# Slot 10 of a main batch: the load of the fourth operand's sums ahead of the loads of the sixth operand and of v

## The chip, the cores and the metric

The kernel runs on one core of one Trainium2 chip. The metric is the device time of the whole program in microseconds (us), the median of several runs. TensorE (PE) does the matrix products, VectorE (DVE), ScalarE (ACT) and GpSimd (POOL) the elementwise work, and SyncE (SP) issues nearly all DMA transfers from one queue that it works through in order.

## What is computed

Attention with a threshold, for 8 batches, 8 heads, 576 positions and head size 64, and behind it a gated feed-forward block over the 4608 tokens that come out:

```python
scores = scale * np.matmul(q, k.transpose(0, 1, 3, 2))
thresh = np.max(scores, axis=-1, keepdims=True) - tau
scores = np.where(scores >= thresh, scores, -1000000000.0)
scores = scores - np.max(scores, axis=-1, keepdims=True)
attn = np.exp(scores)
attn = attn / (np.sum(attn, axis=-1, keepdims=True) + 1e-09)
attn_out = np.matmul(attn, v)                  # (B,H,S,D), then turned to x: (B*S, H*D)
g = x @ w_gate
silu = g * (1.0 / (1.0 + np.exp(-g)))
val = x @ w_val
out = silu * val @ w_out                       # d_model 512, d_ff 1536
```

All numbers are float32.

## The kernel before

**Slots.** From the second batch on the attention of a batch is cut into 12 slots: four pairs of heads with three slots each. The loop at the end of the kernel function counts them with `s`; `b` is the batch, `kk = s % 12` the slot in it, and `x` (0, 1 or 2) the slot within its pair. A slot starts on PE with the scores (`slot_scores`, L1989, written to the tile `sc`). With `x == 1`, PE first multiplies the attention of the pair before with v (`attend`, L2088, tile `xa`). DVE, ACT and POOL find maxima, exponentials, masks, sums and transposes of the scores (`slot_rest`, L2010 to L2066). The rest of PE's time in a slot is filled with the feed-forward part of the batch before (`block_part`): first gates and values (L1109), then the output product.

**The output product from the third chunk on** is the class `Deep`. A product is split by nested schemes of seven products in place of eight, so that operands are sums and differences of blocks. Its steps are spread over slots: `p1` and `gates_end` in slot 9, `p2` and `p7` in slot 10, `p6` and `p4` in slot 11, `p5` in slot 0 and `p3` in slot 1 of the next batch. Each step is one call of `nested` (L1711): seven groups of matmuls into `px` or `py`. The token side has sums that POOL makes from `hall` (L925). On the weight side three of the seven operands have sums that don't fit on the chip. They stand in `stream_hbm` (operands 5, 3 and 4 counted from 0) and are loaded for each chunk by `stream` (L1612). Operand 3, which is the fourth, is the one of this case: `p7` asks for its load, its place is `middle` (a part of the tile `big`), which `p7` itself still reads through the sums of its token side, and `p4` in the next slot multiplies with it. Operand 2 has its sums in `sixth_hbm`; `sixth` (L1617) loads them into `xall`, for `p3`.

**Other loads around it.** `prepare_next` loads q and k of the next pair in slots with `x == 1` (L419, four transfers each); DVE and POOL scale and transpose them (L2138, L2135, L2141), and the scores of the next pair need them two slots later. `prepare_v` loads v of the pair that is in work (`load_v`, L456, four transfers of 144 KB); its reader is `attend` three slots later. A one-element memset on DVE (`clear_first`, L1022) comes ahead of it, and the load waits for that. `ship` stores finished outputs (L1772). `next_flow` loads the weight sums of gates and values for the next chunk (L1040, 1280 or 1024 KB each).

**The order.** The kernel writes each engine's instructions in an order that a small planner finds while the program is built. `Plan.job` takes an engine, an assumed duration and what the job depends on (other jobs, or points of planned time such as `plan.t`); an engine's next job is the one that can start first, by rank and by when it is ready. SP counts as an engine here. A dependency that is only a planned time gives an order and no wait; true waits come from the tiles that are read and written. In slot 10 the calls come in this order: `prepare_next`, `prepare_v`, and then `block_part` with `p2` and `p7`. In `p7`:

```python
mark = plan.t
self.inner_sums(4, self.a21, flow_end, self.ready["s1"], mark)
...
stream(3, False, m)
deep_jobs[2] = sixth(self.c, mark)
```

Here `m` is `mark` and a fixed pipeline time of 0.22. So SP gets, in slot 10: four loads of q, four of k, four of v, one store of outputs, the sixth operand, the fourth operand's sums, and behind them, when PE has done `p6`, the first of the loads L1040.

Of the kernel before, what the change touches and what calls it, by code (L numbers as in the profile page):

```python
# [27 lines left out]
class Plan:  # L28
# [12 lines left out]
    def job(self, eng, took, fn, *deps, rank=1, lag=0.0, moves=0.0):  # L41
        j = Job(eng, took, fn, rank, lag, moves)
        for d in deps:
            if isinstance(d, Job) and d.end is None:
                d.then.append(j)
                j.waits += 1
            elif d is not None:
                j.ready = max(j.ready, self.after(d, eng) if isinstance(d, Job) else d + self.HOP)
        if not j.waits:
            self.open[eng].append(j)  # L50
        return j
# [93 lines left out]
def kernel(  # L145
# [63 lines left out]
    vall = const.tile([P, 2 * NJ * D], F32, name="vall")  # L209
# [641 lines left out]
    plan = Plan()  # L851
# [62 lines left out]
    DEEP = 2  # L914
# [106 lines left out]
    def clear_first(place, *deps):  # L1021
        return job("DVE", 0.07, lambda: nc.vector.memset(place[:, 0:1], 0.0), *deps, rank=0)  # L1022
# [69 lines left out]
    class Group:  # L1092
# [89 lines left out]
        def p7(self):  # L1182
            m = self.mul(self.b, self.w[6], x_block(self.c, 1, 0), False, self.u1, *self.w_deps[6], *ready_x[self.c][3])
            u, old = turn_of(u_bufs)
            self.u2_buf = u
            self.u2 = job("ACT", 0.55, lambda: nc.scalar.activation(u.ap, self.b.rows(), AF.Copy, scale=0.5), m, *old, rank=0)
            tt, eng, took = (dve_tt, "DVE", 0.62) if tail[0] else (pool_tt, "POOL", 1.3)
            self.g2 = job(eng, took, tt(u.ap, u.ap, self.s.ap, ALU.add), self.u2, self.s5, rank=1)
            self.s.jobs = [self.g2]
# [328 lines left out]
    deep_jobs = [[] for _ in operands]  # L1518
# [41 lines left out]
    def sixth_place(c):  # L1560
        return xall[:, c % 2 * XW:(c % 2 + 1) * XW]
# [47 lines left out]
    def stream(o, in_tail, *deps):  # L1609
        w = (2 if o == 4 else 3) * QW  # L1610
        place = place_of(o, in_tail)
        deep_jobs[o] = [thirds[o], job("SP", 0.1, lambda: nc.sync.dma_start(out=place[:, 0:w], in_=stream_hbm[STREAMED.index(o)][:, 0:w]),  # L1612
                                       *streamed_kept[o], *deps, lag=1.6, moves=2.2)]

    def sixth(c, *deps):
        place = sixth_place(c)
        return [*deep_jobs[2][:1], job("SP", 0.1, lambda: nc.sync.dma_start(out=place, in_=sixth_hbm), *sixth_kept, *deps, lag=1.6, moves=1.9)]  # L1617
# [12 lines left out]
    def last_of_sixth(*deps):  # L1630
        b11, b12, b21, b22 = quarters(operands[2])
        deep_jobs[2] = [job("POOL", 1.0, pool_tt(b12, b22, b12, ALU.subtract), *sixth_kept, kept_third[2], *deps, rank=3)]
# [7 lines left out]
    class Deep:  # L1640
# [229 lines left out]
        def p7(self):  # L1870
            self.y, deps = self.pair("py")
            m = self.nested(6, self.y, True, *deps)
            mark = plan.t
            self.inner_sums(4, self.a21, flow_end, self.ready["s1"], mark)
            self.inner_sums(2, self.a12, free_place, self.ready["s4"], m, *(j for x in sevens[False] for j in x.jobs))
            stream(3, False, m)
            deep_jobs[2] = sixth(self.c, mark)
            self.c7 = self.copies(self.spaces[1], self.y, m, *u_list[1].jobs, *u_list[2].jobs, *u_list[3].jobs)

        def p6(self):  # L1880
# [265 lines left out]
    def prepare_v(seg, *deps):  # L2146
        seg["vj"] = job("SP", 1.7, lambda: load_v(seg), *deps, lag=2.3, moves=2.6)
# [42 lines left out]
    def gv_steps(n, before_attend=False):  # L2190
        for x in range(n):
            holding[0] = before_attend and x >= n - (HELD if state["c"] >= DEEP else 2)
            next(state["gv"])
        holding[0] = False

    def out_steps(n):
        for _ in range(n):
            if not state["run"]():
                state["run"] = None

    NS = NU3 * NP
    LAST_GV, LAST_PLAIN = 9, 8
    HELD = 4
    GV = {1: 3, 2: 6, 3: 4, 4: 6, 5: 7, 6: 3, 7: 5, 8: 7, 9: 0}
    GV_FIRST = {1: 5, 2: 8, 3: 2, 4: 5, 5: 7, 6: 2, 7: 5, 8: 7, 9: 0}
# [16 lines left out]
    def block_part(b, kk):  # L2222
        s = (b - 1) * NS + kk
        if s == 0:
            state["gv"] = chain(*(plain_group(0, g, u_bufs) for g in range(IN_HEAD, NF2)), *(plain_group(1, g, n_bufs) for g in range(NF2)))
        if s <= NS:
            gv_steps(PLAIN.get(s, 0))
            if s == 2:
                first, state["run"] = outputs(0)
                first.half_sums(plan.t)  # L2230
            elif s == LAST_PLAIN:
                next(state["gv"], None)
            out_steps(CH0.get(s, 0))
            return
        c = b - 1
        if c == DEEP and kk == 0:
            deepen_sixth(plan.t, *summed)
        if kk < 2 and state["run"]:
            out_steps((CH if c - 1 < DEEP else CD).get(kk, 0))
        if kk in GV:  # L2240
            if kk == 1:
                state["gv"], state["c"] = gates_and_values(c), c
                if c > DEEP:
                    deepen_x(c, *(j for js in streamed_kept.values() for j in js))
            gv_steps((GV_FIRST if c == 1 else GV)[kk], kk % NU3 == 0)
            if c == DEEP and kk == 2:
                for o in (4, 2):
                    keep_third(o, plan.t, *summed)
                last_of_sixth(plan.t)
                for o in STREAMED:  # L2250
                    last_of_streamed(o, plan.t)
            if c == DEEP and kk <= len(NESTED):
                deepen(NESTED[kk - 1], plan.t, *(j for js in plain_stores.values() for j in js), *summed)
            if kk == LAST_GV:
                next(state["gv"], None)
                begin_outputs(c)
                if c < DEEP:
                    out_steps(1)
                    end_gates()
        if kk >= LAST_GV:  # L2260
            out_steps((CH if c < DEEP else CD).get(kk, 0))
# [5 lines left out]
    for s, (n, x) in enumerate((n, x) for n in range(len(halved)) for x in range(NU3)):  # L2267
        seg = halved[n]
        i, t = seg["i"], seg["tiles"][x]
        b, kk = s // NS + 1, s % NS  # L2270
        if x == 1 and n > 0:
            attended = attend(halved[n - 1])
        pss, mark = slot_scores(seg, t)
        if s == 0:
            next(last, None)
            attend_tile()
            next(last, None)
            flip()
            plan.t += 2.4
            plan.free.update(DVE=2.0, ACT=2.5)  # L2280
        elif s == 1:
            box = []
            m = pe(1.0, lambda: attend_tile(lambda *y: box.extend(y)))
            j = job("ACT", 0.27, box[1], m, rank=0)
            banks[taken[id(box[0])][0]].jobs.append(j)
            give_back(box[0])
            next(last, None)
            store_last(0, j)
        if s == 1:
            prepare_v(seg)  # L2290
        at_, pooled, max_by_act = (kk, POOLED, MAX_BY_ACT) if b > DEEP else (s, FIRST_POOLED, FIRST_MAX_BY_ACT)
        slot_rest(seg, t, pss, mark, pooled.get(at_, 0), at_ in max_by_act, 1 if x == NU3 - 1 else 2)
        if x == 1 and n > 0:
            for place, load in held:
                load(clear_first(place, behind_scores[0]))
            held.clear()
        if x == (1 if n >= NP else 0) and n + 1 < len(halved):
            prepare_next(i + 1, plan.t, n >= 2 * NP)
        if x == 1 and n > 0:
            prepare_v(seg, clear_first(vall, attended, behind_scores[0]))  # L2300
        if s == 0:
            joins = rest_of_weights()
        block_part(b, kk)
        if 2 <= s < 6:
            output_sums(s - 2, plan.t, *joins)
        if s in WS:
            g, place = WS[s]
            weight_sums(g, place, plan.t, *joins, stores.get({2: 0, 3: 1, 4: 3, 5: 4}.get(g)))
        if 10 <= s < 10 + NF2:
            g = s - 10  # L2310
            weight_part(g, summed_g[g], plan.t)
        if s > NS and x and (g := (s - NS) * (NU3 - 1) // NU3) < NF2:
            store_plain(g, parts[g], plan.t)
            store_nested(g, plan.t)
        if s in STREAM_AT:
            deepen_streamed(STREAM_AT[s], plan.t, *(j for js in (*plain_stores.values(), *nested_stores.values()) for j in js), *summed)
# [70 lines left out]
```

## Time and profile before

| what | us |
|---|---|
| median of 3 runs | 1353.04 |
| lowest and highest of them | 1350.48, 1359.38 |
| the profiled execution, its own time | 1355.35 |
| its span from first to last instruction | 1353.6 |
| PE busy in the span | 1336.0 |
| DVE, ACT, POOL busy | 1066.3, 894.9, 776.2 |

The profiled execution is 2.31 us above the median of the runs. Its span is 1.75 us shorter than its own time; that is what lies around the first and the last instruction. Engines work beside each other, so the busy times don't add up. An engine line such as `L1711 ... px<-wo,hall` names the line of the kernel, the tile that is written and the tiles that are read. SPq is the stream of DMA issues of SP; the time of such a line is that of the issue, and the time to landing is given apart. A main batch takes about 145.5 us: the scores of slot 10 start at 667.33, 813.08 and 1104.07 us, for instance, in the second, third and fifth of the batches that the change touches.

### The profile page before, as it was taken

The page shows a single profiled execution, that of the slowest core. Times are in us where ns is not written, and L with a number is a line of the kernel's source. Part 1 is how long each engine was busy: PE and PEld are TensorE (multiplying, and loading weights), DVE is VectorE, ACT ScalarE, POOL GpSimd, SP SyncE. Part 2 cuts the span into 40 slices and gives each one's busy share as a digit, 9 for nine tenths or more (in the row PEclk, how much of TensorE's full clock was granted, in tenths as well). Part 3 has the DMA queues.
Part 4 walks back from the last instruction along what each step waited for, and adds up shares of the span by engine and source line. Part 5 has one row for each costly group of instructions (what it writes and reads, how often), then busy time and mean ns, then how long its engine had stood idle before and what let it go on. Part 6 is the DMA issues. An engine that isn't in the chain of part 4 may idle for free.

```text
span 1353.6 us, 40310 instructions
## 1 busy us (share of the span) xinstructions
PE 1336.0 (99%) x15914; PEld 1119.7 (83%) x15914; DVE 1066.3 (79%) x2860; ACT 894.9 (66%) x2315; POOL 776.2 (57%) x870
## 2 busy tenths in 40 slices
PE   9999999999999999999999999999999999999998
PEld 7777777787788878888888888887888889999998
DVE  7788898878887787888878887888788876686686
ACT  6888776777755777677767776778677774330330
POOL 2687397565685659655984689556965595000000
PEclk9999999999999999999999999999999999999999
DMA  8753324456557544746264636563464627524621
GB/s 190 194 184 100 75 61 130 127 150 174 149 180 219 174 109 107 213 131 194 60 197 148 211 97 194 158 212 71 145 202 132 185 65 251 201 96 168 207 83 31
DMA packets 216140, 202.11 MB, mean 149 GB/s; under 512 B 166800, under 2 KB 184208, under 8 KB 205200
## 3 DMA queue, kind: packets, MB, share of 16 engines
q1 hardware_dynamic: 212032, 198.62, 49.6%
q8 instruction: 126, 2.06, 0.6%
q10 hardware_dynamic: 3920, 0.92, 0.3%
q14 instruction: 62, 0.51, 0.1%
HBM read 172.36 MB, written 27.13 MB: 147 GB/s over the span
## 4 chain that ended last, share of the span: by engine, by line
PE 86%; POOL 6%; DMA 3%; DVE 2%; issue 1%; SPq 1%; ACT 0%; DVEq 0%; POOLq 0%
PE pb L1109 18%; PE pa L1109 12%; PE sc L1989 9%; PE xa L2088 9%; PE px L1711 9%; PE pe L1109 6%; PE po L1416 6%; PE pe L1294 4%; DMA big<-stream_hbm 2%; PE py L1711 2%; PE pv L1341 2%; POOL big L925 2%; PE pg L1341 2%; PE sc L1294 2%; POOL hall L925 2%; PE py L1720 2%
## 5 line engine op out<-in xcount | busy, mean ns | idle before, releaser
L2037 DVE SCALAR_TENSOR_TENSOR pall<-sc,th,pall 128x288 f32<-128x288 f32 x504 | 244.5, 514 | 41.7 <-ACT pall L2035 22.5
L1109 PE MATMUL pb<-xall,big 128*128 128x256 f32 x1152 | 273.9, 381 | 0.0
L2035 ACT ACTIVATE pall<-sc,nm 128x288 f32<-128x288 f32 x504 | 232.5, 497 | 33.3 <-DVE pall L2037 33.0
L1109 PEld LDWEIGHTS pb<-xall,big 128*128 128x128 f32 x1152 | 215.0, 190 | 30.7 <-issue 2.7
L2066 DVE STREAM_TRANSPOSE pall<-pall 128x576 f32<-128x576 f32 x252 | 188.4, 764 | 23.6 <-ACT pall L2064 15.6
L2064 ACT ACTIVATE pall<-pall,ri 128x288 f32<-128x288 f32 x388 | 179.0, 527 | 33.9 <-DVE ri L2052 33.0
L1109 PE MATMUL pa<-xall,big 128*128 128x256 f32 x768 | 183.1, 381 | 0.0
L925 POOL TENSOR_TENSOR hall<-hall,tmp 128x512 f32<-128x512 f32 x80 | 102.1, 1278 | 106.7 <-DVE hall L1164 87.0
L1109 PEld LDWEIGHTS pa<-xall,big 128*128 128x128 f32 x768 | 143.3, 190 | 21.6 <-issue 2.5
L2010 DVE TENSOR_REDUCE mx<-sc 128x2 f32<-128x576 f32 x168 | 126.0, 750 | 43.8 <-PE sc L1989 43.3
L925 POOL TENSOR_TENSOR big<-big 128x128 f32<-128x128 f32 (+3 forms) x174 | 128.7, 747 | 44.0 <-ACT big L1216 22.4
L1989 PE MATMUL sc<-kT,qT 64*32 64x288 f32 (+1 forms) x5376 | 144.8, 345 | 1.1 <-DVE pall L2037 1.1
L1989 PEld LDWEIGHTS sc<-kT,qT 64*32 64x32 f32 x5376 | 95.3, 106 | 50.0 <-issue 9.3
L2088 PE MATMUL xa<-pall,vall 64*32 64x288 f32 x4032 | 128.8, 404 | 0.4 <-PE px L1711 0.4
L2088 PEld LDWEIGHTS xa<-pall,vall 64*32 64x32 f32 x4032 | 75.5, 107 | 46.0 <-issue 4.0
L2061 POOL TENSOR_SCALAR pall<-pall,ri 128x288 f32<-128x288 f32 x116 | 58.4, 515 | 73.0 <-DVE ri L2052 71.1
L1109 PE MATMUL pe<-xall,big 128*128 128x256 f32 x384 | 91.4, 381 | 0.0
L2046 ACT COPY sums<-sums 32x6 f32<-32x6 f32 x336 | 66.6, 198 | 30.2 <-DVE pall L2037 26.1
L1163 ACT ACTIVATE vall<-tmp 128x512 f32<-128x512 f32 x96 | 59.9, 627 | 37.1 <-POOL tmp L925 17.3
L1109 PEld LDWEIGHTS pe<-xall,big 128*128 128x128 f32 x384 | 72.4, 190 | 11.1 <-ACT pall L2064 1.1
L2012 DVE TENSOR_REDUCE mx<-sc 128x1 f32<-128x288 f32 x168 | 75.2, 447 | 0.0
L925 POOL TENSOR_TENSOR big<-hall 128x384 f32<-128x384 f32 (+2 forms) x69 | 65.2, 970 | 14.7 <-PE pa L1109 14.6
(290 smaller groups left out, 2631.7 us busy)
## 6 DMA issues: line engine op xcount, KB each, us to landing
big<-sums_hbm SPq DMA_DIRECT2D x42, 1280.0 KB, 6.7
big<-sums_hbm SPq DMA_DIRECT2D x42, 1024.0 KB, 6.8
vall<-in_v_dram SPq DMA_DIRECT2D x112, 144.0 KB, 3.4
sums_hbm<-big SPq DMA_DIRECT2D x36, 256.0 KB, 3.9
out_dram<-big SPq DMA_DIRECT2D x32, 256.0 KB, 3.5
qT<-in_q_dram SPq DMA_DIRECT2D x112, 72.0 KB, 4.0
kT<-in_k_dram SPq DMA_DIRECT2D x112, 72.0 KB, 3.0
wo<-in_moe_w_gate_dram SPq DMA_DIRECT2D x16, 384.0 KB, 3.6
```

The lines of the kernel that those rows point to most:

```text
L925: return lambda: nc.gpsimd.tensor_tensor(out=out, in0=a, in1=b, op=op)
L1109: nc.tensor.matmul(ps[:, i], w[:, k_, i * P:(i + 1) * P], x[:, k_, :], start=first and i == k_ == 0, stop=True, skip_group_check=True)
L1294: nc.tensor.matmul(self.es[b_].ap()[:, at_ * P:(at_ + 1) * P], ws[n], xd[o][n], start=b_ not in begun, stop=True, skip_group_check=True)
L1416: nc.tensor.matmul(ps, h(f), w[:, f, :], start=(f == 0), stop=(f == NF2 - 1))
L1711: nc.tensor.matmul(ps, a[:, f, :], ws[n][:, f, :], start=bank_ not in begun, stop=True, skip_group_check=True)
L1989: nc.tensor.matmul(pss[h][(slice(g * G, (g + 1) * G), *part)], qT[hs, col:col + G], kT[hs, c * SH + keys[0]:c * SH + keys[1]], start=True, ...
L2010: rs.append(job("DVE", 0.72, lambda n=n, tile_=tile_: nc.vector.tensor_reduce(out=mx[:, n:n + 2, 0], in_=tile_[:, :, 0:SH], axis=AX.X, op= ...
L2035: ej = job("ACT", 0.42, lambda x=x, n=n: nc.scalar.activation(ps[x], scs[x], AF.Exp, bias=nm[:, n:n + 1]), ej, masks.get((h, u - 1)), rank=0)
L2037: masks[x] = job("DVE", 0.45, lambda x=x, n=n: nc.vector.scalar_tensor_tensor(out=ps[x], in0=scs[x], scalar=th[:, n:n + 1], in1=ps[x], op0 ...
L2064: scaled.append(job("ACT", 0.46, lambda x=x, n=n: nc.scalar.activation(x, x, AF.Copy, scale=ri[:, n:n + 1]), rj, rank=rank))
L2066: seg["turned"].append(job("DVE", 0.72, lambda both=both: nc.vector.transpose(out=both, in_=both), *scaled, rank=rank))
L2088: nc.tensor.matmul(holds[a].ap()[x * G:(x + 1) * G, 0:SH].rearrange("d (i q) -> d i q", q=G), vr[rs, h, j, ds], p[rs, h, :, j, :], start=( ...
```

## The change

In slot 10 of the batches from `b == 3` on, of which there are five, `prepare_v` is called behind `block_part` in place of ahead of it, with a planned time a little behind `p7` as a further dependency. In `p7`, the load of the sixth operand gets a planned time 0.3 behind that of the fourth operand's sums. What each operation does is unchanged.

```diff
@@ class Deep, p7
             stream(3, False, m)
-            deep_jobs[2] = sixth(self.c, mark)
+            deep_jobs[2] = sixth(self.c, m + 0.3)
@@
-    LAST_GV, LAST_PLAIN = 9, 8
+    LAST_GV, LAST_PLAIN, LATE_V = 9, 8, 10
@@ the loop over slots
-        if x == 1 and n > 0:
+        late_v = kk == LATE_V and b > DEEP
+        if x == 1 and n > 0 and not late_v:
             prepare_v(seg, clear_first(vall, attended, behind_scores[0]))
         if s == 0:
             joins = rest_of_weights()
         block_part(b, kk)
+        if late_v:
+            prepare_v(seg, clear_first(vall, attended, plan.t + plan.PIPE + 0.3))
```

In the order of instructions that comes out, PE, ACT and POOL have the same instructions in the same order as before. On DVE, the memset L1022 moves in each of the five slots from behind the first maxima (L2010 and L2012) to behind the reciprocal L2052. On SP the order in each of the five slots changes so (`x2` and `x4` count transfers):

```
before                                     after
L456  vall<-in_v_dram      x4              L1772 out_dram<-big
L1772 out_dram<-big                        L1612 big<-stream_hbm
L1617 xall<-sixth_hbm                      L1617 xall<-sixth_hbm
L1612 big<-stream_hbm                      L456  vall<-in_v_dram      x4
L1040 big<-sums_hbm        x3              L1040 big<-sums_hbm        x3
```

## The prediction

> **What bounds the kernel now.** I read the page first (busy times, the chain that ended last), then PE's waits, then the order of time of SP, PE, DVE and POOL around the third slot 10 that the change touches (815 to 865 us).
>
> ```profile
> span 1353.6 us, 40310 instructions
> PE 1336.0 (99%) x15914; PEld 1119.7 (83%) x15914; DVE 1066.3 (79%) x2860; ACT 894.9 (66%) x2315; POOL 776.2 (57%) x870
> ```
>
> PE is busy for 1336.0 of 1353.6 us. Whatever is done to loads, no more than the 17.6 us between them can go, 1.3%. So the question is which part of them this change reaches.
>
> ```profile
> PE py L1711 <- DMA big<-stream_hbm: 4.5, 4, 1.5
> PE sc L483 <- DVE pall L507: 2.8, 4, 1.1
> PE idle L290 <- DVE pall L272: 1.3, 1, 1.3
> PE sc L1989 <- DVE pall L2037: 1.1, 1, 1.1
> ```
>
> The first row of PE's waits is `p4` waiting for the fourth operand's sums: four times, 4.5 us. Asked for each batch alone, PE has no other wait in the four batches from 510 to 1093 us. So these 4.5 us are all that PE can gain there.
>
> ```profile
> 817.05 1.96 SPq L419 DMA_DIRECT2D qT<-in_q_dram  x4
> 819.10 3.29 SPq L419 DMA_DIRECT2D kT<-in_k_dram  x4
> 822.50 1.96 SPq L456 DMA_DIRECT2D vall<-in_v_dram  x4
> 824.57 0.41 SPq L1772 DMA_DIRECT2D out_dram<-big  x1
> 825.02 0.47 SPq L1617 DMA_DIRECT2D xall<-sixth_hbm  x1
> 825.59 0.43 SPq L1612 DMA_DIRECT2D big<-stream_hbm  x1
> 831.15 6.01 SPq L1040 DMA_DIRECT2D big<-sums_hbm  x3
> ```
>
> The columns are start and duration of the issues. From 817 us SP issues without a pause; the stream load is the last in the row, behind 576 KB of v, 256 KB of output and 512 KB of the sixth operand.
>
> ```profile
> 822.18 1.50 PE L1711 MATMUL py<-big 128*128 128x128 f32 x12
> 823.52 0.83 PE L1711 MATMUL py<-extra,big 128*128 128x128 f32 x6
> 833.41 0.91 PE L1711 MATMUL py<-big,hall 128*128 128x128 f32 x6 [1.19 <-DMA big<-stream_hbm]
> 836.93 1.72 PE L1989 MATMUL sc<-kT,qT 64*32 64x288 f32 x64
> 843.46 4.59 PE L2088 MATMUL xa<-pall,vall 64*32 64x288 f32 x144
> ```
>
> PE could have gone on at 833.41 - 1.19 = 832.22 us. The first line is the last read of the place that the stream load overwrites; v is read at 843.46 only.
>
> ```profile
> 823.61 0.19 DVE L2052 RECIPROCAL ri<-tot 128x6 f32<-128x6 f32 x1
> 824.99 0.78 DVE L2138 STREAM_TRANSPOSE kT<-kT 128x576 f32<-128x576 f32 x1 [1.19 <-DMA kT<-in_k_dram]
> 834.25 0.78 DVE L2141 STREAM_TRANSPOSE qT<-qT 128x576 f32<-128x576 f32 x1
> 837.04 0.69 DVE L1955 TENSOR_TENSOR vall<-py,vall 128x512 f32<-128x512 f32 x1 [2.02 <-PE py L1711]
> ```
>
> The k load has landed by 824.99. DVE then has 2.02 us idle ahead of the add that takes `p4`'s result.
>
> **The change part by part.** Nothing is removed or added; in each of five slots six issues change places (one stream, one sixth, four v) and one memset moves.
>
> *The stream load goes ahead.* In the four slots it was issued at 535.72, 680.45, 825.59 and 971.18 us and took 6.42, 7.43, 7.69 and 7.69 us to land; PE waited 0.42, 1.53, 1.19 and 1.38 us, in sum 4.52. Behind the k loads now come the store (0.45 with its gap) and then the stream. What holds it is PE's last read of its place, which ends at 533.30, 677.94, 823.68 and 969.08 us (start and 1.50 of the group shown, and of its like in the other slots). In the fifth slot no q and k loads are in front: there that read ended at 1113.18 + 1.50 = 1114.68 and the stream issue stands at 1114.84, 0.16 later. With 0.16 the issues come to 533.46, 678.10, 823.84 and 969.24, which is 2.26, 2.35, 1.75 and 1.94 us earlier than before. SP is free in time: in the third slot k ends at 822.39 and the store is issued by about 823.3 (its DVE producer ends at 822.83).
>
> *How long it then takes to land* no row shows for this order. From above it is the old 7.69, though less is in front; from below the 4.9 of the fifth slot (with a store and the sixth in front, but no q and k). I take about 6, between them: the k loads are there by 824.99, and v and the sixth are gone from the front. Either end has the same result. With the old landing times the sums are there at 539.88, 685.53, 831.53 and 976.93; PE wants them at 541.85, 686.48, 832.22 and 977.63. The narrowest margin is 0.69 us, with 4.9 it is 3.5. So the wait goes in all four: -4.52 us. In the fifth slot there was none to win: 0.
>
> *What is late next.* PE comes to the scores of slot 0 earlier, in the third slot at 835.74. They need the transpose of q, which hangs on the slot before and doesn't move: it ends at 834.25 + 0.78 = 835.03, 0.71 ahead. In the other three the same sum gives 0.71 or 0.72. The add on DVE and what follows (sums, scaling on ACT, transposes for `xa`) hang on `p4`'s end and move with it: DVE has 2.02 us idle there. POOL waits 1.17 us for that add at 837.81 and has its own work done at 836.63, so its sums move by 1.17 of 1.19; `p5` reads the last of them at 842.70, 2.2 us after they are ready at 840.46. Cost: 0.
>
> *The sixth operand* is issued right behind the stream, about 0.7 us earlier than before, and read at 850.92: 0.
>
> *The loads of v* move behind store, stream and sixth. They start at about 823.84 + 0.43 + 0.57 = 824.9 and not at 822.5, and take 1.96 us of SP, so SP is done at about 826.9. Queued behind them is the first of the loads L1040, which waits for `p6` and is issued at 831.15 only: 4.2 us of cover. The second of them waits for the stream's landing (7.0 us in SP's waits), which now comes earlier. Each v piece landed in 2.9 to 3.7 us, and the longest anywhere took 6.7; from 826.5 that is 833.2 at the worst, 9 us ahead of `xa` at 842.27. Cost: 0. If that cover were gone, `xa` and all behind it on PE would wait 1 us for each us of delay.
>
> *The memset* takes 0.06 us. It lands between the reciprocal (ends 823.80) and the k transpose (824.99), in 1.19 us of idle time, and the v loads behind it in SP's queue come later than it. From below it gives the maxima 0.01 us (the start of what follows), from above it costs 5 x 0.06 = 0.3 us: I take 0.
>
> The sum is -4.52 us. The profiled execution's 1355.35 becomes 1350.8, its span 1349.1. That execution was 2.31 above the median of the runs, so for the median I say 1353.04 - 4.52 = 1348.5 us.
>
> **A rule beside it.** The Trainium skill, in "DMA: Bandwidth & Descriptors", section "Queues, rings and completion order", says that a DMA's semaphore increment lands only after every earlier write of the same DMA engine. By that rule the v data in front were part of the 7.69 us. The same page, under "Specifications", gives 512 B as the least size for full rate, and that speaks against the change: the q and k loads, which stay in front, would then be what is slow. By that the landing time would stay at 7.69 and the sum would still be -4.52, with the margin of 0.69 us. The trace here has 166800 of 216140 packets under 512 B, and the k loads landed by 824.99.
>
> **The rivals.**
>
> *The stream is late all the same.* For it: landing took longest where q and k were in front (6.42 to 7.69 against 4.9). Against: k is there by 824.99. It needs a landing time over 7.69 + 0.69 in the third slot; if none of the wait goes, the time is 1353.0.
>
> *Another wait takes its place.* After the move, q's transpose is only 0.71 us ahead of the scores. If what hangs on the new order comes 0.71 + 0.6 us later than I work out, half of the gain goes: 1353.04 - 2.3 = 1350.8. Against: nothing that q's transpose hangs on is moved.
>
> *Slower: v comes too late.* SP works in order, so v now hangs on the store and on PE's last read of the stream's place. It decides from a delay of 9 us beyond my 826.9 on; 13 us in each of five slots would cost 5 x 4 = 20 us and give 1373. For it: in other slots SP has waited up to 18.3 us in front of a v load, for the memset. Against: the memset in these slots stands behind a reciprocal that ends 19.7 us ahead of `xa`, and PE's reads are done by 824.
>
> *The change doesn't do what it says* is excluded: SP's order has the stream ahead of v in all five slots.
>
> **How the numbers follow.** All four waits go, 1348.5: 0.79. The stream is late all the same, 1353.0: 0.09. Another wait, 1350.8: 0.07. v too late, 1356 and up: 0.05. The range adds to the likeliest case how the runs of before scatter (1350.48 to 1359.38 about 1353.04; less for a median of three, about 3 us) and reaches over the first two rivals: 1345.0 to 1354.0. About 1% is what a measurement of this kernel can tell from no change, 13.5 us. Faster by over 1% would need three quarters of all that PE is ever idle, 17.6 us: 0.02. Slower by over 1% is the greater part of the last rival: 0.04. Within 1%: 0.94.
>
> **What would show it.** Right: PE's waits have no row for `stream_hbm`, the stream load is issued some 0.2 us behind the end of PE's read of its place and lands in 5 to 7.5 us, the scores of slot 10 in the second and the third of these batches stand 145.75 - 1.53 = 144.2 us apart, `xa` waits for no v, and DVE's idle time ahead of L1955 is shorter by what PE gained. Wrong: a remaining wait of `p4`, a new wait of the scores L1989 for DVE, of `xa` for v, or of the gates L1109 for L1040's loads.

## The result, and the profile after

| | before | after |
|---|---|---|
| median of 12 runs, us | 1354.11 | 1350.74 |
| lowest and highest run | 1350.48, 1359.38 | 1348.60, 1351.43 |
| the profiled execution, its time | 1355.35 | 1349.87 |
| its span | 1353.6 | 1348.0 |

The ratio of the mean times is 0.9971, with a 95% interval of 0.9959 to 0.9984: 3.9 us less, between 2.2 and 5.6; the medians lie 3.4 us apart. The runs after also lie closer together, 2.8 us from lowest to highest where the runs before had 8.9.

The page of the changed kernel, first two lines:

```profile
span 1348.0 us, 40299 instructions
PE 1334.6 (99%) x15914; PEld 1118.9 (83%) x15914; DVE 1066.5 (79%) x2860; ACT 895.7 (66%) x2315; POOL 778.0 (58%) x870
```

PE has the same matmuls to do; what is gone is time between them. PE's waits in the changed kernel, longest first:

```profile
PE sc L483 <- DVE pall L507: 3.0, 5, 1.0
PE idle L290 <- DVE pall L272: 1.3, 1, 1.3
PE sc L483 <- DVE cap L719: 1.3, 1, 1.3
PE sc L1989 <- DVE pall L2037: 1.0, 1, 1.0
```

The row for `stream_hbm`, 4.5 us before, is gone, and no new row took its place. All waits that are left lie ahead of 140 us or in the tail, at 1126 us. SP in the third of the changed slots (start and duration of the issues):

```profile
816.59 3.67 SPq L419 DMA_DIRECT2D kT<-in_k_dram  x4
820.36 0.57 SPq L1772 DMA_DIRECT2D out_dram<-big  x1
821.24 0.35 SPq L1612 DMA_DIRECT2D big<-stream_hbm  x1
821.65 0.45 SPq L1617 DMA_DIRECT2D xall<-sixth_hbm  x1
822.19 2.83 SPq L456 DMA_DIRECT2D vall<-in_v_dram  x4
828.70 4.55 SPq L1040 DMA_DIRECT2D big<-sums_hbm  x3
```

PE at the same place:

```profile
819.67 1.50 PE L1711 MATMUL py<-big 128*128 128x128 f32 x12
...
821.78 1.72 PE L1989 MATMUL sc<-kT,qT 64*32 64x288 f32 x64
...
829.55 0.83 PE L1711 MATMUL py<-big,hall 128*128 128x128 f32 x6
...
833.00 1.72 PE L1989 MATMUL sc<-kT,qT 64*32 64x288 f32 x64
839.53 4.59 PE L2088 MATMUL xa<-pall,vall 64*32 64x288 f32 x144
```

The stream load is issued at 821.24, 0.07 us after PE's last read of its place (819.67 + 1.50 = 821.17), so it can't go earlier. The trace gives it 6.4 us to landing. PE goes from one group of `p4` to the next without a wait. DVE:

```profile
821.07 0.19 DVE L2052 RECIPROCAL ri<-tot 128x6 f32<-128x6 f32 x1
821.27 0.06 DVE L1022 MEMSET vall<- 128x1 f32 x1
822.64 0.78 DVE L2138 STREAM_TRANSPOSE kT<-kT 128x576 f32<-128x576 f32 x1 [1.31 <-DMA kT<-in_k_dram]
831.74 0.77 DVE L2141 STREAM_TRANSPOSE qT<-qT 128x576 f32<-128x576 f32 x1
833.11 0.69 DVE L1955 TENSOR_TENSOR vall<-py,vall 128x512 f32<-128x512 f32 x1 [0.59 <-PE py L1711]
```

The memset stands in idle time, as worked out. DVE's idle time ahead of the add L1955 is 0.59 us where it was 2.02. The transpose of q ends at 832.51, 0.49 us ahead of the scores.

**What the four slots lost.** The scores of slot 11 and of slot 0 frame the place where PE waited. In the changed kernel their starts lie 11.22 us apart in all four slots (833.00 - 821.78 in the third). What the distance is longer by in another kernel is what the slot lost there, whatever the wait rows say. In the third slot of the kernel before, PE's scores of slot 11 and its last group ahead of the wait were these (the scores of slot 0 start at 836.93):

```profile
824.28 1.72 PE L1989 MATMUL sc<-kT,qT 64*32 64x288 f32 x64
...
830.72 1.50 PE L1711 MATMUL py<-extra,hall 128*128 128x128 f32 x12
```

For the kernel before the distance gives 0.66, 1.77, 1.43 and 1.61 us, 5.47 in sum, where its wait rows had 4.52. The two agree on the place and not on the size: each slot lost 0.23 to 0.24 us more than its row. In the third slot: PE's group of 12 starts at 830.72, the next would start 1.34 later at 832.06 (as 822.18 is followed by 823.52), but the row counts idle time from the modelled end at 832.22, which is 0.16 late; and the group behind the wait took 0.91 and not 0.83.

From slot 1 of the first of these batches to the end the changed kernel keeps its lead: 0.75, 2.51, 3.93 and then 5.55 us behind the four slots, 0.08 of it from what lies ahead of 510 us.

### The profile page after: what moved, and what is told of

It is laid out like the page before. It is cut to its first block, busy times and chain, and to the rows that moved or that the text cites. A ratio compares the mean times of both kernels' runs of the same rounds, so it can differ in the third digit from the quotient of the medians.

```text
span 1348.0 us, 40299 instructions
## 1 busy us (share of the span) xinstructions
PE 1334.6 (99%) x15914; PEld 1118.9 (83%) x15914; DVE 1066.5 (79%) x2860; ACT 895.7 (66%) x2315; POOL 778.0 (58%) x870
## 4 chain that ended last, share of the span: by engine, by line
PE 93%; DVE 2%; DMA 2%; POOL 1%; ACT 1%; issue 1%; SPq 0%; ACTq 0%; DVEq 0%; POOLq 0%
PE pb L1109 19%; PE pa L1109 13%; PE px L1711 12%; PE sc L1989 10%; PE xa L2088 9%; PE pe L1109 6%; PE po L1416 6%; PE pe L1294 4%; PE py L1711 3%; PE pv L1341 2%; PE pg L1341 2%; PE sc L1294 2%; PE py L1720 2%; PE sc L483 1%; PE pv L600 1%; DMA wo<-in_moe_w_gate_dram 1%
## 5 line engine op out<-in xcount | busy, mean ns | idle before, releaser
L2010 DVE TENSOR_REDUCE mx<-sc 128x2 f32<-128x576 f32 x168 | 125.9, 750 | 43.4 <-PE sc L1989 42.8
L2012 DVE TENSOR_REDUCE mx<-sc 128x1 f32<-128x288 f32 x168 | 75.0, 446 | 0.0
```

What stands on the lines that cost most here:

```text
L2010: rs.append(job("DVE", 0.72, lambda n=n, tile_=tile_: nc.vector.tensor_reduce(out=mx[:, n:n + 2, 0], in_=tile_[:, :, 0:SH], axis=AX.X, op= ...
```

## The experiments

All times below are compared with runs of the kernel before in the same session (median 1353.45 us in 21 runs for the first four, 1353.86 in 7 for the others).

### Stream ahead of the sixth operand, v still in front

```diff
-            deep_jobs[2] = sixth(self.c, mark)
+            deep_jobs[2] = sixth(self.c, m + 0.3)
```

> One part alone: the stream load goes ahead of the sixth operand's load, v stays in front of both. In the third slot the stream issue should come 0.57 us earlier than before (the sixth's issue and gap), with 512 KB less in front of it. Theory (what is in front, in issues and in data, sets the landing): the change as a whole cut the landing from 7.69 to 6.4 us by taking 1088 KB out of the front, so 512 KB is worth about 0.6, and the sums land about 1.2 us earlier than before. The slots lost 0.66, 1.77, 1.42 and 1.61 us by the distance of the scores; of that 0.66 + 3 x 1.2 = 4.2 goes, and PE keeps a wait of a few tenths in three slots. Rival (only v in front matters): the issue alone moves, 0.57 in each slot, 2.2 us in all, and the waits stay near 0.6 to 1 us.

Measured: 1350.37 us, ratio 0.9982 (0.9973 to 0.9991). The slots lost 0.21, 0, 0 and 0 us. PE's waits have no row for `stream_hbm`. SP in the third slot:

```profile
820.69 1.98 SPq L456 DMA_DIRECT2D vall<-in_v_dram  x4
822.76 0.41 SPq L1772 DMA_DIRECT2D out_dram<-big  x1
823.28 0.40 SPq L1612 DMA_DIRECT2D big<-stream_hbm  x1
823.73 0.48 SPq L1617 DMA_DIRECT2D xall<-sixth_hbm  x1
```

The stream took 7.0, 4.8, 6.4 and 5.9 us to land, against 6.42, 7.43, 7.69 and 7.69 before: in three slots 1.3 to 2.6 us less, in the first 0.6 more. Even with v in front the wait goes all but completely. The slots lost 5.3 us less than in the profiled execution of before, but that one lost more than two others did (below), and by the ratio the gain is between 1.2 and 3.7 us. So the theory's 4.2 was counted on too large a loss, and the time alone doesn't rule out the rival's 2.2. The landing speaks for the theory: counted from the scores of slot 11, the sums are there after 7.0 us on average, against 8.4 in the three profiles of before. That is 1.4 us earlier, near the 1.2 of the theory and not the 0.57 of the issue alone.

### v behind, the sixth operand still ahead of the stream

Its diff is that of the change without its first part: `sixth(self.c, mark)` stays.

> The other part alone: v goes behind, the sixth operand stays in front of the stream load. The issue of the stream should be where it is in the changed kernel (PE's last read of its place holds it), only with 512 KB more in front. Theory (data in front count): it lands about 0.6 us later than in the changed kernel, 5.5 to 7 us after its issue, still ahead of PE, so no wait of p4 is left and the time is that of the changed kernel, 5.5 us less in the span than before. Rival (only the place of the issue counts): it lands in 4.9 to 6.4 us as in the changed kernel; same time. Rival (the sixth is the one that hurts): landing goes back to about 7.7 and waits of some tenths come back.

Measured: 1349.57 us, ratio 0.9974 (0.9965 to 0.9983). The slots lost 0, 0, 0.27 and 0 us. SP in the third slot:

```profile
819.82 0.41 SPq L1772 DMA_DIRECT2D out_dram<-big  x1
820.27 0.47 SPq L1617 DMA_DIRECT2D xall<-sixth_hbm  x1
820.85 0.38 SPq L1612 DMA_DIRECT2D big<-stream_hbm  x1
821.33 2.13 SPq L456 DMA_DIRECT2D vall<-in_v_dram  x4
```

Here the issue comes 0.1 to 0.4 us later than in the changed kernel, counted from the scores of slot 11, and it took 7.2, 7.6, 8.3 and 5.5 us to land; in the changed kernel 5.6, 4.9, 6.4 and 5.7. The 512 KB of the sixth operand in front do count, by 1.6 to 2.7 us in three slots, where the theory had 0.6; in the fourth they don't. In the third they bring back 0.27 us. The last rival came nearest: the landing is about that of before (6.3 to 7.7 in its three profiles), and what v's move gains is the issue, 1.7 to 2.2 us earlier behind the scores. So either part alone takes nearly all of the wait, in its one profile and by its median, and the second one adds margin. It can be put in one sum: take the landing of the stream from the start of slot 11's scores. PE needs it 829.55 - 821.78 = 7.77 us behind them.

| third slot | issued | to landing | behind the scores | lost |
|---|---|---|---|---|
| before | 825.59 | 7.69 | 9.00 | 1.43 |
| sixth behind the stream | 823.28 | 6.4 | 7.42 | 0 |
| v behind | 820.85 | 8.3 | 7.88 | 0.27 |
| both (the change) | 821.24 | 6.4 | 5.86 | 0 |

(The scores start at 824.28, 822.26, 821.27 and 821.78.) What is over 7.77, and about 0.2, is what the slot loses: 9.00 - 7.77 + 0.2 = 1.43, and 7.88 - 7.77 + 0.2 = 0.31 against 0.27.

### v loaded twice in the order of before

```diff
-        seg["vj"] = job("SP", 1.7, lambda: load_v(seg), *deps, lag=2.3, moves=2.6)
+        def load():
+            for _ in range(2 if twice else 1):
+                load_v(seg)
+
+        seg["vj"] = job("SP", 1.7, load, *deps, lag=2.3, moves=2.6)
```

`twice` holds in the five slots.

> The suspected cost doubled: the order of before, but in the five slots each load of v is issued twice, 576 KB and 2 us of SP's time more in front of the stream load (the second load writes the same data again). Theory: the sums land 2.0 to 2.7 us later than before in the four slots with q and k in front, and PE loses as much more in each: 8 to 11 us in all, about 1363, slower by 0.6 to 0.8%; nothing in the fifth slot. The row of PE's waits should again come out about 0.24 us a time below what the distance of the scores shows. Rival (v in front is hidden and something else held the stream): no more than 2 us in all.

Measured: 1371.95 us (1367.09 to 1376.06), ratio 1.0141 (1.0113 to 1.0168). SP in the third slot, and a row of SP's waits for the whole program:

```profile
828.35 5.36 SPq L456 DMA_DIRECT2D vall<-in_v_dram  x8
833.76 0.42 SPq L1772 DMA_DIRECT2D out_dram<-big  x1
834.23 1.46 SPq L1617 DMA_DIRECT2D xall<-sixth_hbm  x1
835.79 0.38 SPq L1612 DMA_DIRECT2D big<-stream_hbm  x1
SPq L456 <- DMA vall<-in_v_dram: 8.9, 17, 1.3
```

The landing behind the scores is 10.86, 11.69, 11.05 and 11.08 us, 1.9 to 2.6 later than before. That is the size that was expected, but not by the way that was expected. Each piece of the second load goes to the place of the same piece of the first, and SP waits for that one to land: in the third slot the first pieces land at 831.40, 832.10, 832.67 and 833.38, and the second ones are issued at 831.46, 832.16, 832.68 and 833.40. So v holds SP for 5.4 us and not 4, the stream is issued 3.1 to 4.4 us later behind the scores than before, and it then takes only 5.3 to 6.5 us to land. The run shows what a late place in the queue costs; it doesn't show that more data in front make the landing longer.

By the sum above the slots should lose 3.3, 4.1, 3.5 and 3.5. They lost 3.31, 5.72, 3.47 and 5.11. The time that is too much in the second and the fourth shows for the second in these windows (length, busy time of PE, PEld, DVE, ACT and POOL, then the granted clock of PE, DMA share, GB/s):

```profile
686.00:692.00 6.00, 2.28 (x21) 2.09 (x19) 4.81 (x15) 3.83 (x11) 6.00 (x7) 1.00 0.88 309
692.00:694.00 2.00, 1.86 (x12) 1.89 (x13) 0.00 (x0) 0.00 (x0) 0.71 (x1) 0.72 0.92 389
694.00:696.00 2.00, 2.00 (x11) 2.00 (x11) 0.00 (x0) 0.00 (x0) 0.00 (x0) 0.50 0.09 36
696.00:698.00 2.00, 2.00 (x35) 1.65 (x41) 0.61 (x2) 0.00 (x0) 0.00 (x0) 0.92 0.36 61
```

PE waited 3.85 us here, and behind the wait its granted clock is 0.50 for 3.4 us, from 692.9 to 696.3: a group of matmuls that takes 1.50 elsewhere took 2.54. So the size that was expected (1363) fell short, by a cost that has nothing to do with the loads: a wait that is long enough is paid again in clock. The four runs bear this out: from the fastest to the slowest (1367.09, the profiled one, 1369.61, 1374.29, 1376.06) their mean granted clock is 0.997, 0.996, 0.994 and 0.993.

### v moved on to the end of slot 11

```diff
         if late_v:
-            prepare_v(seg, clear_first(vall, attended, plan.t + plan.PIPE + 0.3))
+            waiting_v = seg, attended
+        elif kk == LATE_V + 1 and b > DEEP:
+            prepare_v(waiting_v[0], clear_first(vall, waiting_v[1], plan.t + plan.PIPE + 0.3))
```

> The changed kernel with v moved further, to the end of slot 11, behind the three loads L1040 that p6 and p4 ask for; this tries the rival that ended slower. In the third slot the last L1040 is issued at about 832.8 us of the changed kernel's time and xa starts at 839.5. Theory (v has some 6 us of cover and no more): v is issued from 833 on with 3.6 MB in front and lands at 842 to 845, so xa waits 3 to 5 us in each of five batches: 1366 to 1376, slower by over 1%. Rival (a v load that comes late is still hidden): no wait of xa, about 1351. The planner also moves some DVE and ACT instructions around it, which may cost or gain some tenths.

Measured: 1384.54 us (1381.55 to 1390.4), ratio 1.0241 (1.0215 to 1.0266). PE's waits:

```profile
PE xa L2088 <- DMA vall<-in_v_dram: 17.8, 4, 5.2
PE xa L2088 <- ACT sums L2046: 4.4, 1, 4.4
```

The five waits are those of `xa`, 4.1 to 5.2 us each (the second row is the first batch, where v's landing is put down to an engine that had long been done). In the third batch v is issued from 848.46 on and takes 9 us, and the scores behind `xa` start 6.24 us later than in the changed kernel (17.16 behind those of slot 0, not 10.92), and those of the slot after it another 0.43: the wait of 4.30, and a clock of 0.50 behind it from 858.7 to 862.0 us. So the slower rival is a real one. The wait is about what v came too late by (`xa` was due 17.75 us behind the scores of slot 11, at 853.67, and v's last piece landed at 858.64), and the clock comes on top: the five waits are 22.2 us in sum, which would give the 1366 to 1376 that were expected, and the profiled execution took 1384.32. The change stays clear of it. In the changed kernel the last piece of v landed 6.3, 9.3, 8.2, 6.3 and 8.5 us ahead of `xa` in the five slots: a cover of 6.3 us at the least.

### q and k behind the stream as well

```diff
-            prepare_next(i + 1, plan.t, n >= 2 * NP)
+            if not (kk == LATE_V and b > DEEP):
+                prepare_next(i + 1, plan.t, n >= 2 * NP)
...
         if late_v:
+            if n + 1 < len(halved):
+                prepare_next(i + 1, plan.t + plan.PIPE + 0.3, False)
             prepare_v(seg, clear_first(vall, attended, plan.t + plan.PIPE + 0.3))
```

> The changed kernel with the loads of q and k also behind the stream and the sixth operand (ahead of v) in the five slots; the first memsets of their tiles are left out. Theory (in the four slots the stream's landing time of 4.9 to 6.4 us comes from what is in front): with only the store in front it lands in about 3.8, as in the fifth slot of the changed kernel; PE gains nothing by it, since it waits no more there. q and k come 6 to 8 us later, the transpose of q on DVE ends after PE is ready for the scores of slot 0, and PE waits 1 to 5 us in each of four slots: 1355 to 1371. Rival: the transposes of q and k still keep ahead of the scores, 1350.7 as in the changed kernel.

Measured: 1365.55 us (1364.73 to 1371.17), ratio 1.0099 (1.0074 to 1.0124). The stream landed in 4.1 to 4.2 us in the slots where the trace has it. PE and DVE at the start of slot 0 in the first batch:

```profile
548.15 1.23 PE L1989 MATMUL sc<-kT,qT 64*32 64x288 f32 x25 [3.02 <-issue]
```

```profile
545.16 0.69 DVE L1955 TENSOR_TENSOR vall<-py,vall 128x512 f32<-128x512 f32 x1 [1.28 <-PE py L1711]
...
546.61 0.78 DVE L2138 STREAM_TRANSPOSE kT<-kT 128x576 f32<-128x576 f32 x1
547.31 0.73 DVE L2141 STREAM_TRANSPOSE qT<-qT 128x576 f32<-128x576 f32 x1
```

The transpose of q ends at 548.04, and the scores follow at once; each of the four slots lost 3.09 or 3.10 us. (The row names no releaser; the transpose that ends just ahead of it is what it needs.) So q and k in front of the stream are worth 1.4, 0.8 and 2.2 us of its landing time in the first three slots, and this order pays more for it than it gets. But the transposes don't follow the landing at once: q has landed by 541.73 and k by 544.38. The planner has put both transposes behind the adds L1955 and L1957, which hang on `p4`, and the scaling of q on POOL behind other sums, at 545.42. An order that transposes k in the 1.28 us of DVE's idle time wasn't tried, so the run doesn't show how late q and k may come.

### The kernel before, profiled twice more

> The kernel before once more, for the size of the gain: its profiled execution lost 5.46 us in the four slots by the distance of the scores, while the medians of before and after lie 3.4 us apart. Theory: the stream's landing, and with it the wait, varies from run to run, and the profiled execution of before (1355.35, with a median of 1354.11) had more of it than the usual one; then a run at 1352 to 1354 has losses of 2.5 to 4.5 us in sum, and losses and time move together. Rival: the losses are 5.4 us again whatever the time, and what differs between runs lies elsewhere.

> The same as the run ahead of it, for a second point: by the theory its time less its losses in the four slots is the same as that of the other profiled runs of before and after, within 1 us; by the rival the losses stay at 5.4 us and the rest moves.

Measured, with the losses from the distance of the scores:

| profiled execution | time, us | lost in the four slots | sum | time less sum | behind `after` near 510 us | time less both |
|---|---|---|---|---|---|---|
| before, as predicted from | 1355.35 | 0.66, 1.77, 1.43, 1.61 | 5.47 | 1349.88 | 0.08 | 1349.80 |
| before again | 1353.2 | 0.03, 0.83, 0.62, 1.14 | 2.62 | 1350.58 | 0.76 | 1349.82 |
| before a third time | 1350.6 | 0, 1.09, 0.50, 0.26 | 1.85 | 1348.75 | -1.13 | 1349.88 |
| after | 1349.87 | 0, 0, 0, 0 | 0 | 1349.87 | 0 | 1349.87 |

The loss itself varies between runs of one kernel, by 3.6 us here, and the sum with 7.77 gives each of these losses to within 0.03 us from the landing. The time less the losses lies within 1.8 us and not within the 1 us that was expected. What is over was there before these batches began: the sixth column gives how much later than in the changed kernel the scores of slot 9 in the first of them start, near 510 us. Without that too, the four lie within 0.1 us of each other, and so do the two runs with half of the change (1349.89 and 1349.81). So in these six executions nothing else on PE's way differs by more than that. PE's wait rows for the second execution show less than it lost, and put a part down to ACT:

```profile
PE py L1711 <- ACT pall L2035: 1.0, 2, 0.6
PE py L1711 <- DMA big<-stream_hbm: 0.9, 1, 0.9
```

So the theory of the size holds, with the start of the program as a second thing that varies: the profiled execution that the prediction was made from had more of this wait than most, and a gain of 5.5 us there goes with 3.4 us between the medians.

No run pointed to a version faster than the changed kernel: with the wait gone, PE has none left in these batches that a load could take away.

## Why the prediction was right

- *The place and the cause.* The wait of `p4` was all there was to win in these batches, and it went in four of four slots, while all else took the same time to within 0.1 us. The stream came first into the queue and was held by PE's last read of its place alone, 0.07 us behind it (0.16 was taken).
- *The landing time.* About 6 us was taken, between 4.9 and 7.69; 5.6, 4.9, 6.4 and 5.7 were measured. They didn't stay at the old 7.69 with q and k in front, whose share was 0.8 to 2.2 us. It was said that even the old landing times would do. With v behind alone they came back (7.2 to 8.3), and three slots of four lost nothing. The margin of 0.69 us in the third was about 0.5, since PE was ready at 832.06 and not at 832.22, and 8.3 us to landing used it up.
- *What was late next.* q's transpose still came in time, with 0.49 us to spare and not 0.71; the difference is the 0.24 us by which the slot gained more than its wait row. POOL's wait for DVE's add, 1.17 us before, is gone with the rest.
- *v.* It cost nothing, as said. But the bound was too tight: the pieces took 6.2 to 9.5 us to land behind store, stream and sixth operand, and 6.7 was taken as the worst. The cover was 6.3 us and not 9. When v was moved on beyond it, PE paid.
- *The size.* The sum was -4.52 us, and two errors in it partly hid each other. The wait rows understate what PE lost, so the profiled execution's own gain is 5.47 (its time went from 1355.35 to 1349.87, where 1350.8 was forecast). And that execution was not a usual one: it was corrected for by the 2.31 us that it lay above the median of three runs, but the term that was removed was itself part of why it lay above. With 12 runs the medians differ by 3.4 us. The forecast 1348.5 is 2.2 us low, inside its range: 1.15 us because the usual run had less to win than 4.52, and 1.07 because the median of three runs, 1353.04, was that much below the median of twelve. The range, 1345 to 1354, was wide enough to hold no gain at all (1353.04), so the number alone says little; the place of the wait and its going are what bear the forecast out.
- *The rivals.* The stream late all the same: seen for 0.27 us in one slot, and only with half of the change. Another wait in its place: not seen, and that its 1350.8 is the time that came out is an accident; one appears when q and k are moved as well, in the order that the planner then finds. v too late: real, from about 6 us of further delay on.

By the rule in "DMA: Bandwidth & Descriptors" of the Trainium skill (section "Queues, rings and completion order"), earlier writes of the same DMA engine hold up a DMA's semaphore. Three slots of four agree in that 512 KB more in front cost 1.6 to 2.7 us; in the fourth they cost nothing.

## What to carry to other kernels

When one queue issues loads in order, sort them by when their reader needs them and not by when they can start; here a load that PE needed 8 us behind the scores of slot 11 stood behind one that it needed 18 us behind them. Move one only as far as its own reader leaves room, and count that room with the landing time that it will have in its new place, not in its old one. And size a wait by the distance between two fixed points on the engine that waits, in more than one run: the row of the wait, and the one profiled run, can each be off by a good part of it.

## What the runs showed of the hardware that was not expected

- **A wait of PE of 3 us or more can cost half as much again.** At waits of 3.85 and 3.25 us (v loaded twice) and 4.1 to 5.2 us (v at the end of slot 11) the granted clock fell to 0.50, for 3.4 us, or 6.8 at two of the latter; at waits of 3.07 and 3.24 us it did not. Of the four waits of 3.02 us with q and k late, one was followed by it (the next scores came another 1.8 us later), three were not. What decides is how the wait lies in time: within each trace the changes of the clock stand a multiple of 3.41 us apart. Cut into stretches of 3.41 us by that grid, the stretch ahead of a fall held 2.24 us or more of PE's idle time at each of the eight waits with a fall, and none of the stretches at the five waits without one held more than 1.95. (One fall near 118 us, long before these slots, followed a stretch with 1.07 us.) The Trainium skill, in "TensorE: Matmul & The Clock Gate", Part 1, gives an idle window of about 3.4 us that runs freely. The grid of 3.41 us in these traces agrees with it; but the window needn't be idle from end to end, as 2.24 us in it were enough.
- **A load's time to landing depends on what is under way in front of it, and not on the bytes in front alone.** The same 576 KB took 4.1 to 4.2 us with a store in front, 4.9 to 6.4 with q and k, and 7.2 to 8.3 in three slots of four (5.5 in the fourth) with the sixth operand as well. With v loaded twice it had the most data in front, but was issued later, when the first load of v had landed: 5.3 to 6.5. In one kernel, that of before, the same slot's landing differed by up to 1.3 us between three profiles. v's pieces of 144 KB took 2.6 to 3.7 us in the place that they had before and 6.2 to 9.5 behind.
